# A written order for every engine in place of the planner's, in a kernel of linear attention and a gated feed-forward block

## The chip, the core and the metric

One core of a Trainium2 chip runs the whole kernel. The metric is the device time of one execution in microseconds (us). The engines are TensorE (PE in the profile, its weight loads PEld), VectorE (DVE), ScalarE (ACT), GpSimd (POOL) and SyncE (SP), which here only issues DMA transfers. Each works through its own list of instructions in order; between engines, semaphores say when data are there or a buffer is free.

## The reference, cut to what matters

```python
def _attn_ref(q, k, v, g_norm):              # (8, 8, 576, 64) each
    kv = np.einsum('bhsd,bhse->bhde', k, v)
    out = np.einsum('bhsd,bhde->bhse', q, kv)
    rms = np.sqrt(np.mean(out * out, axis=-1, keepdims=True) + 1e-06)
    return (out / rms * g_norm)

def _moe_ref(x, w_in, w_spatial, b_spatial, w_out):   # x (8, 576, 512)
    h = np.maximum(x @ w_in, 0.0)                     # w_in (512, 1024)
    u, v = (h[..., :512], h[..., 512:])
    v_n = (v - v.mean(-1)) / np.sqrt(v.var(-1) + 1e-06)
    v_s = np.einsum('ts,bsd->btd', w_spatial, v_n) + b_spatial[None, :, None]
    return (u * v_s) @ w_out                          # w_out (512, 512)
```

The attention's output, heads side by side, is the x of the second function. All is float32.

## The kernel before, in words

The eight batches are worked one after the other. A batch has 576 rows: four blocks of 128, and a tail of 64 rows; the tails of two batches share one block. Products in full precision are made from a high and a low part of each operand (`XH`, `XL`, `WVH`, ...; `split`, L508 and L509, casts the high part on ScalarE and subtracts it on VectorE), three TensorE products for one. Large products are cut into halves and put together as in Strassen's scheme (seven products for eight), whose sums and differences VectorE makes.

From batch 2 on a batch b has these stages on TensorE:

- `hv` (L505, tiles `psh`): v half of x @ w_in, four blocks, each followed by ReLU (L478), the layer norm's statistics (L484 to L491), scaling on ScalarE (L492) and a split into `VH`, `VL`. The tail's block is `hv_tail`, split into `TA` and `TB` (L554 to L556).
- `u_steps` (L697 to L727, tiles `psua`, `psub`, `psuc`, products at L742): the u half of x @ w_in. Its step p1 is copied out of PSUM by ScalarE (L697, `p`), since p2 goes on in the same bank; p7 adds it on VectorE (L716, `u`), and p4 goes on in that bank.
- `sp_steps` (L790 to L811, tiles `psa`, `psb`, `psc`): the product with w_spatial, in the same pattern (the copy is L790), then `gate` (L761, L763), which multiplies by u and splits the result into `G`, `GT`.
- `out_unit` (L472 with tiles `pso` and operands `WO`, `G`): the product with w_out, a copy by ScalarE (L844) and a store (L846).

The attention of a later batch is woven in: `part_k` (L300, `pskv`) makes kv from loads of `KV` and `KT`; `part_q` (L329, `pso` from `KVB` or `KVO` and `qt`) applies it to the queries; `square` (L372 to L375) and `normal` (L383, `x`) do the norm out of PSUM; `turn_over` (L407, `pstr`) transposes into `XH`, `XL` (L239, L240). These products use the array in pieces of 64x64 or 64x128 (the first pair of numbers in a profile row), all others use it whole, 128*128. A product in plain float32 shows as two records in the trace, one on split operands as one.

What sets the order: the source emits 5,750 instructions, and a planner then lists each engine's in an order of its own, by its estimate of when each could start, within what data and buffers allow. The token list `PLAN` sets the order in which the opening is emitted (pinned between its brackets), and `tc.issue_after` and `tc.high_priority` bind a few instructions; one such bond ties `x_sums` of a batch to the last `gate` of the batch before (L625 to L628, L766). PSUM has four banks for the main products (`ps_mm`) and two double banks for the attention (`ps_att`); `load` has two buffers for `qt` and `qs`, and `KV`, `KT` are pairs.

Of the kernel before, what the change touches and what calls it, by code (L numbers as in the profile page):

```python
# [39 lines left out]
u10 b1 X2 B10 t1 W W E1 L E0 A11 u11 W Q0 z u12 h D12 u13 W B12 T10 s s | s X1 T12 X0 s B11 D13 X5  # L40
B13 T11 X7 s s s s Y1 Y0 X4 P T13 O0 Q1 X6 W | p O1 R
"""


def f32(ap):
    return ap.bitcast(F32)
# [3 lines left out]
def body(ctx: ExitStack, tc, qT, qtl, kvm, kvt, g2, w_in, wsT, bsp, w_out, out):  # L50
    nc = tc.nc
# [455 lines left out]
    def split(hi, lo, x):  # L507
        nc.scalar.copy(hi, x)  # L508
        nc.vector.tensor_tensor(lo, x, f32(hi), op=ALU.subtract)  # L509
# [114 lines left out]

    def x_sums():  # L625

        with tc.issue_after(last_gate[0]):
            x_sums_()  # L628

    def x_sums_():  # L630
        for k in range(2):
            q = []
            for of, j, name in ((0, 0, "p1"), (2, 1, "u2"), (0, 1, "u3"), (2, 0, "g")):
                q.append(work.tile([P, HS], F32, name=name, tag=name))
                x = [f32(x[:, of + k, j * HS:(j + 1) * HS]) for x in (XH, XL)]
                nc.vector.tensor_tensor(q[-1], *x, op=ALU.add)
            q11, q22, q12, q21 = q
            nc.vector.tensor_tensor(q11, q12, q11, op=ALU.subtract)
            nc.vector.tensor_tensor(q12, q22, q12, op=ALU.subtract)
            nc.vector.tensor_tensor(q22, q22, q11, op=ALU.subtract)  # L640
            nc.vector.tensor_tensor(q21, q21, q22, op=ALU.subtract)
            for n, x in (1, q22), (0, q11), (2, q12), (3, q21):
                split(TH[n][:, k], TL[:, n, k], x)
# [106 lines left out]
        nc.tensor.matmul(ps, TB[i][:, ds], WTL[i][:, cols], start=False, stop=True,  # L750
                         skip_group_check=True)

    last_gate = [None]

    def gate(b, d, j, ps, add=None):

        i = b % 2
        cols = slice(j * HS, (j + 1) * HS)
        g = work.tile([P, HS], F32, name="g", tag="g")
        if add is not None:  # L760
            nc.vector.tensor_tensor(g, ps, add, op=ALU.add)  # L761
            ps = g
        nc.vector.scalar_tensor_tensor(g, U[:, d, cols], 0.0, ps, op0=ALU.max, op1=ALU.mult)  # L763
        if j == 0:
            split(GH[:, d, cols], GL[:, d, cols], g)
            last_gate[0] = next(i for i in reversed(nc.cur_bb.bb.instructions) if i.engine == mybir.EngineType.DVE)  # L766
        else:
            n, own = NT - HS, slice(i * TAIL, (i + 1) * TAIL)
            split(GH[:, d, HS:NT], GL[:, d, HS:NT], g[:, 0:n])
            split(GT[:, 0, d, own], GT[:, 1, d, own], g[:, n:HS])  # L770

    def sp_steps(b):
# [29 lines left out]
        def p2(q):  # L802
            ps = st.pop((q, "a"))
            product(ps, q, 1, 1, False, False)
            tail_product(ps, i, q, 0)
            gate(b, q, 0, ps)

        def p7(q):
            ps = st[q, "b"]
            product(ps, q, 4, 5, False)  # L810
            nc.vector.tensor_tensor(temp(q, "u3"), ps, st[q, "p1"], op=ALU.add)  # L811
            gate(b, 2 + q, 1, st[q, "c"], st.pop((q, "u3")))

        def p4(q):
            ps = st.pop((q, "b"))
            product(ps, q, 2, 6, False, False)
            tail_product(ps, i, 2 + q, 0)
            gate(b, 2 + q, 0, ps, st.pop((q, "p1")))
# [220 lines left out]
    def step(n=1):  # L1039
        for _ in range(n):  # L1040
            if queue:
                queue.pop(0)()
# [98 lines left out]
    def first(b):  # L1141

        if b > 1:
            to_u()
            x_sums()
# [48 lines left out]
    for b in range(2, NB):  # L1194
# [5 lines left out]
        if b % 2 == 0:  # L1200
            step(len(queue))


_OUTS = [((B, S, DM), "float32")]

# [43 lines left out]
```

## Time and profile before

| what | value |
|---|---|
| median of 3 runs | 524.04 us (522.02 to 526.14) |
| the profiled execution | 522.39 us |
| its span, first to last instruction | 520.6 us |
| its mean granted TensorE clock | 0.99 of 2.4 GHz |

The profile comes from one execution. An engine's busy time is a union of its instructions; matmuls are pipelined, so the busy time of PE contains overlap and small gaps. A wait is named by what ended it.

### The profile page before, as it was taken

What the parts mean: (1) busy time and instruction counts of PE and PEld (TensorE: products, weight loads), DVE (VectorE), ACT (ScalarE), POOL (GpSimd) and SP (SyncE); (2) the same over time, 40 slices, a digit from 0 to 9 for tenths busy, and PEclk for the clock granted to TensorE, in tenths of its full rate; (3) what the DMA queues carried; (4) which work ended last, traced back from release to release, by engine and by line L of the source; (5) the groups of instructions that cost most, each with busy time, mean ns of one, the idle gap of its engine ahead of it and who ended that gap; (6) DMA issues with size and microseconds to landing.
All of it is one profiled execution on the core that took longest, in us unless ns stands there. A gap on an engine that the chain in (4) does not pass through costs nothing.

```text
span 520.6 us, 12023 instructions
## 1 busy us (share of the span) xinstructions
PE 488.3 (94%) x4560; PEld 422.3 (81%) x4560; DVE 412.1 (79%) x1248; ACT 282.6 (54%) x913; POOL 20.7 (4%) x46
## 2 busy tenths in 40 slices
PE   6999999979799978999999999899999998999896
PEld 6658697867697868888988888788998888989895
DVE  2899888889597498796989689797899589876871
ACT  3758946865352675525653476435664377326422
POOL 5000000000000001000000000100000001000000
PEclk9999999998999979999999999999999999999999
DMA  7995100775526603817063153816050151214303
GB/s 251 336 349 209 40 3 20 238 235 168 161 89 195 226 1 115 313 54 251 13 228 108 50 173 93 296 40 212 2 196 11 49 175 55 108 42 162 137 26 103
DMA packets 28079, 71.99 MB, mean 138 GB/s; under 512 B 3506, under 2 KB 8626, under 8 KB 26484
## 3 DMA queue, kind: packets, MB, share of 16 engines
q1 hardware_dynamic: 24564, 49.19, 28.9%
q0 software_dynamic: 3456, 22.02, 12.3%
q8 instruction: 36, 0.59, 0.4%
q14 instruction: 23, 0.19, 0.1%
HBM read 58.09 MB, written 13.11 MB: 137 GB/s over the span
## 4 chain that ended last, share of the span: by engine, by line
PE 65%; DVE 12%; DMA 12%; ACT 6%; issue 2%; SPq 1%; ACTq 0%; DVEq 0%
PE pso L472 16%; PE psh L505 12%; PE psa L742 5%; PE psub L742 5%; DMA qt<-qT 4%; PE psua L742 3%; PE psb L742 3%; PE psc L742 3%; PE psuc L742 3%; PE psh L559 3%; DMA out<-o 2%; PE pso L329 2%; DMA stage<-w_out 2%; DMA spare_u<-w 2%; DMA KV<-kvm 2%
## 5 line engine op out<-in xcount | busy, mean ns | idle before, releaser
L472 PE MATMUL pso<-WO,G 128*128 128x512 f32 x384 | 95.1, 395 | 0.0
L472 PEld LDWEIGHTS pso<-WO,G 128*128 128x128 f32 x384 | 70.9, 189 | 14.8 <-ACT o L844 0.4
L508 ACT CAST G<-g 128x288 fp32r<-128x288 f32 (+1 forms) x56 | 22.9, 409 | 58.8 <-DVE g L763 58.5
L505 PE MATMUL psh<-WVH,XH 128*128 128x512 f32 x112 | 43.4, 392 | 0.8 <-ACT XH L239 0.8
L505 PE MATMUL psh<-WVL,XH 128*128 128x512 f32 x112 | 43.6, 390 | 0.0
L505 PE MATMUL psh<-WVH,XL 128*128 128x512 f32 x112 | 42.8, 391 | 0.0
L509 DVE TENSOR_TENSOR VL<-v,VH 128x512 fp32r<-128x512 f32 (+1 forms) x56 | 33.9, 621 | 9.1 <-ACT VH L508 8.6
L844 ACT COPY o<-pso 128x512 f32<-128x512 f32 x35 | 19.7, 590 | 39.2 <-PE pso L472 25.6
L508 ACT CAST VH<-v 128x512 fp32r<-128x512 f32 (+1 forms) x56 | 30.8, 564 | 9.4 <-DVE v L537 8.4
L492 ACT ACTIVATE v<-v,mv,rv 128x512 f32<-128x512 f32 x29 | 23.5, 816 | 22.3 <-DVE mv L491 21.3
L742 PE MATMUL psb<-WSH,VH 128*128 128x288 f32 x84 | 26.6, 317 | 1.9 <-DVE g L763 1.4
L484 DVE BATCH_NORM_STATS2 s<-v 128x6 f32<-128x512 f32 x35 | 23.6, 688 | 5.6 <-ACT v L478 5.4
L239 ACT ACTIVATE XH<-pstr,gcol 128x512 fp32r<-128x512 f32 x28 | 19.4, 704 | 13.5 <-PE pstr L246 6.7
L505 PEld LDWEIGHTS psh<-WVH,XH 128*128 128x128 f32 x112 | 21.0, 188 | 5.6 <-ACT XH L239 1.0
L509 DVE TENSOR_TENSOR G<-g,G 128x288 fp32r<-128x288 f32 (+1 forms) x56 | 23.6, 421 | 2.3 <-ACT G L508 1.8
L742 PE MATMUL psb<-WSH,VL 128*128 128x288 f32 x84 | 24.6, 296 | 0.3 <-DVE VL L509 0.3
L742 PE MATMUL psb<-WSL,VH 128*128 128x288 f32 x84 | 24.7, 295 | 0.0
L505 PEld LDWEIGHTS psh<-WVL,XH 128*128 128x128 f32 x112 | 21.0, 188 | 4.5 <-DVE WVL L904 0.2
L505 PEld LDWEIGHTS psh<-WVH,XL 128*128 128x128 f32 x112 | 21.0, 188 | 4.5
L478 ACT ACTIVATE v<-psh 128x512 f32<-128x512 f32 x32 | 18.7, 599 | 10.1 <-PE psh L505 9.4
L240 DVE SCALAR_TENSOR_TENSOR XL<-pstr,gcol,XH 128x512 fp32r<-128x512 f32 x28 | 20.8, 743 | 2.8 <-ACT XH L239 2.8
L742 PE MATMUL psa<-WSH,VH 128*128 128x288 f32 x56 | 17.4, 312 | 3.4 <-ACT p L790 3.0
(295 smaller groups left out, 1419.6 us busy)
## 6 DMA issues: line engine op xcount, KB each, us to landing
KV<-kvm SPq DMA_DIRECT2D x31, 512.0 KB, 5.5
WO<-spare_o POOLq DMA_DIRECT2D x12, 1024.0 KB, 6.7
UX<-spare_u POOLq DMA_DIRECT2D x12, 768.0 KB, 6.3
out<-o SPq DMA_DIRECT2D x32, 256.0 KB, 2.4
qt<-qT SPq DMA_DIRECT2D x28, 256.0 KB, 4.8
stage<-w_in SPq DMA_DIRECT2D x8, 512.0 KB, 6.9
KT<-kvt SPq DMA_DIRECT2D x32, 64.0 KB, 4.9
stage<-w_out SPq DMA_DIRECT2D x4, 512.0 KB, 5.1
```

Source lines behind the costliest of these rows:

```text
L239: nc.scalar.activation(hi, ps, AF.Copy, scale=gcol)
L240: nc.vector.scalar_tensor_tensor(lo, ps, gcol, f32(hi), op0=ALU.mult, op1=ALU.subtract)
L472: nc.tensor.matmul(ps, lt, rh, start=i == 0, stop=i == n - 1)
L478: nc.scalar.activation(v, ps, AF.Relu)
L484: nc.vector.bn_stats(s6, v)
L492: nc.scalar.activation(v, v, AF.Identity, bias=m, scale=r)
L505: nc.tensor.matmul(ps, lt, rh, start=k == 0 and i == 0, stop=k == NP - 1 and i == 2)
L508: nc.scalar.copy(hi, x)
L509: nc.vector.tensor_tensor(lo, x, f32(hi), op=ALU.subtract)
L559: nc.tensor.matmul(psv[c], X32[:, k, c * P:(c + 1) * P], W32[k], start=k == 0, stop=k == NP - 1)
L742: nc.tensor.matmul(ps, lt, rh, start=start and i == 0, stop=stop and i == len(pairs) - 1, skip_group_check=True)
L844: nc.scalar.copy(o, ps)
```

## The change

A dictionary `ORDER` holds one text for each engine. After all instructions have been emitted as before, the code goes through each text and binds each instruction behind the one that the text puts ahead of it, so that the planner is left with one order for each engine. The bond between `x_sums` and the last gate is taken out. Tiles, buffers, arithmetic, the instructions and the way they wait for data are the same.

```diff
+ORDER = {
+    "PE": """
+0.101 5.20 0.5 6 0.6 7.24 0.7 2.4 0.7 11 14 25 0 10 12 22 0 9 10 0 8.2 16.2 0.8 4.4 0.15 7 20.6 0.5 2.11 4.6
...
+    "Pool": """
+0.6 2.2 4.2 0.8 2 1 0.3 1 0 1 0 2 1 0.3 1 0.6 1 0 1 0
+""",
+}
...
     def x_sums():
 
-        with tc.issue_after(last_gate[0]):
-            x_sums_()
-
-    def x_sums_():
...
-    last_gate = [None]
...
-            last_gate[0] = next(i for i in reversed(nc.cur_bb.bb.instructions) if i.engine == mybir.EngineType.DVE)
...
+    queues = {}
+    for ins in list(nc.cur_bb.bb.instructions):
+        if not isinstance(ins, mybir.BassTilePoolBoundary):
+            queues.setdefault(ins.engine, []).append(ins)
+    for name, text in ORDER.items():
+        left, last = queues[getattr(mybir.EngineType, name)], None
+        for token in text.split():
+            at, n = (int(x) for x in (token + ".1").split(".")[:2])
+            for ins in left[at:at + n]:
+                if last is not None:
+                    tc.add_manual_dep(
+                        ins, last.name,
+                        mybir.DependencyInfo(mybir.DependencyClass.NoSync,
+                                             mybir.DependencyReason.DATA), reason="order")
+                last = ins
+            del left[at:at + n]
```

How a text is read: take the engine's instructions in the order in which the source emits them. A token `a.n` takes n instructions from place a of what is left, and they come next; a token `a` takes one. So `0.101` is the first 101 products as emitted, and `5.20` then takes 20 from five places on. The texts cover all 3,510 products, 760 ScalarE and 1,248 VectorE instructions, 189 issues of SyncE and 43 of GpSimd.

Read out in this way and laid against the order before, the first 340 products, 165 ScalarE and 212 VectorE instructions stand where they stood; product 340 starts at 81.51 us before. Behind that, 1,695 of the 3,510 products would have to be moved to turn the one order into the other. Some places, counted from 0 on each engine (batch numbers from 0):

| engine, what | order before | order in the table |
|---|---|---|
| PE, `part_q` of batch 2, first half | 521 to 552 | 494 to 525 |
| PE, `part_k` of batch 3, first half | 595 to 630 | 607 to 642 |
| PE, `part_q` of batch 2, second half | 631 to 662 | 643 to 674 |
| PE, between the first and the last of these three | 33 products of 288 columns, 9 of 512, `part_k` | 60 of 288, 21 of 512, `part_k` |
| DVE, the four L383 of that first half | 285 to 288 | 277, 280, 283, 284 |
| DVE, a weight's decoding, L895 to L898 | 277, 280, 282, 284 | 285, 286, 288, 290 |
| ACT, two L697 of batch 2 | 315, 319 | 301, 307 |
| ACT, two L492 of `hv` just ahead of the first L697 | 310, 311 | 292, 302 |
| PE, p1 of batch 2, second half; then its p2 | 1116 to 1121; 1160 to 1165 | 1037 to 1042; 1054 to 1059 |
| PE, products between these two | 6 of 288, two `turn_over` | 11 of 512 |
| DVE, two L716 of batch 2 | 478, 479 | 459, 464 |
| DVE, the tail's two L556 of batch 2 | 476, 477 | 468, 473 |
| ACT, two L790 of batch 6 | 689, 690 | 684, 689 |
| ACT, six casts L554 and L555, then L239 and L269 | 681 to 686, 687, 688 | 666 to 672, 700, 686 |
| SP, second `KV` load for `part_k` of batch 2, second half | 62, behind a load of w_out and four stores | 57, ahead of these |
| PE, `part_q` of batch 3, both halves | 892 to 923, 1011 to 1042 | 962 to 993, 1168 to 1199 |
| PE, `hv` of batch 2 starts at | 1050 | 950 |
| PE, `hv` of batch 3 starts at | 1570 | 1354 |
| PE, first `part_k` woven into batch 3 (for batch 4) | 1190 to 1225, in batch 2 | 1470 to 1505 |
| PE, `out_unit` of batch 2, its last product | 1569 | 1397 |
| SP, loads `KV`, `KT`, `qt` for it; the four stores of batch 2 | 115 to 120; 131 to 133, 136 | 119 to 124; 115 to 118 |
| PE, changes of the array's shape behind product 340 | 80 | 51 |

## Rows read from the trace of the kernel before

**Rows 1.** The page, part 1: busy time, share of the span and count of instructions of the engines.

```profile
PE 488.3 (94%) x4560; PEld 422.3 (81%) x4560; DVE 412.1 (79%) x1248; ACT 282.6 (54%) x913; POOL 20.7 (4%) x46
```

**Rows 2.** The waits of TensorE's products alone, from 81.5 us to the end (what waited <- what ended the wait: us in total, times, longest). The ten largest.

```profile
PE pso L329 <- DVE x L383: 3.7, 1, 3.7
PE psua L742 <- ACT p L697: 3.1, 2, 1.8
PE pso L329 <- DMA qt<-qT: 3.1, 3, 1.4
PE psa L742 <- ACT p L790: 3.0, 3, 1.3
PE psub L742 <- DVE u L716: 1.7, 2, 1.3
PE psb L742 <- DVE g L763: 1.4, 2, 1.2
PE pskv L300 <- DMA KV<-kvm: 1.2, 1, 1.2
PE pso L329 <- DVE KVB L317: 1.1, 1, 1.1
PE pstr L407 <- DVE KVO L317: 0.9, 1, 0.9
PE psh L505 <- ACT XH L239: 0.8, 1, 0.8
```

**Rows 3.** Busy time of each engine by stretch: the stretch, its length, busy us and (x instructions) of PE, PEld, DVE, ACT and POOL, then the granted clock of TensorE as a share of its full 2.4 GHz, the share of the DMA engines, GB/s.

```profile
81.50:120.00 38.50, 32.81 (x497) 29.06 (x495) 34.62 (x105) 26.44 (x77) 0.00 (x0) 0.97 0.49 162
...
192.00:196.00 4.00, 4.00 (x17) 4.00 (x17) 3.46 (x11) 2.60 (x7) 0.00 (x0) 0.50 0.00 0
```

**Rows 4.** The chain that ended last, in order of time (start, us, what). A matmul's name is followed by how many of it the piece holds.

```profile
117.92 1.99 PE pso L329 x64
119.90 4.40 PE pso L472 x15
...
190.40 1.81 PE psua L742 x6
192.21 1.59 PE psub L742 x6
193.81 1.44 PE psuc L742 x6
...
229.74 1.21 PE pskv L300 x72
...
237.89 10.90 PE psh L505 x48
248.79 1.58 PE psua L742 x12
...
273.87 1.28 PE pso L329 x64
...
327.35 9.64 DMA qt<-qT
```

**Rows 5.** The timeline of TensorE from 98 to 122 us (start, length of the merged piece, engine, line, what, shape, count, and in brackets the idle time before it).

```profile
98.63 0.29 PE L472 MATMUL psu<-XH,WUL 128*128 128x288 f32 x1
98.85 0.69 PE L300 MATMUL pskv<-KV 64*64 64x64 f32 x32
...
99.59 0.40 PE L472 MATMUL psu<-XH,WUH 128*128 128x288 f32 x1
99.83 0.29 PE L472 MATMUL psu<-XL,WUH 128*128 128x288 f32 x1
...
105.30 1.10 PE L329 MATMUL pso<-KVB,qt 64*64 64x64 f32 x62
...
117.92 1.99 PE L329 MATMUL pso<-KVB,qt 64*64 64x64 f32 x64 [3.67 <-DVE x L383]
```

**Rows 6.** The timeline of VectorE from 113.5 to 118 us.

```profile
115.18 0.43 DVE L897 TENSOR_SCALAR t<-stage 128x512 uint32<-128x512 uint32 x1
...
115.64 0.69 DVE L898 SCALAR_TENSOR_TENSOR stage<-stage,t 128x512 f32<-128x512 uint32 x1
116.25 1.41 DVE L383 TENSOR_TENSOR x<-pso,r 128x256 f32<-128x256 f32 x4
```

**Rows 7.** The timeline of ScalarE from 183 to 190.5 us.

```profile
186.90 0.38 ACT L697 COPY p<-psua 128x288 f32<-128x288 f32 x1
188.28 0.81 ACT L492 ACTIVATE v<-v,mv,rv 128x512 f32<-128x512 f32 x1 [1.00 <-DVE mv L491]
...
189.96 0.39 ACT L697 COPY p<-psua 128x288 f32<-128x288 f32 x1
```

**Rows 8.** The timeline of ScalarE from 438.9 to 442.8 us.

```profile
440.65 0.40 ACT L555 CAST TB<-d 64x256 fp32r<-64x256 f32 x1
...
441.95 0.70 ACT L790 COPY p<-psa 128x288 f32<-128x288 f32 x2
```

**Rows 9.** The timeline of VectorE from 197.5 to 202.2 us.

```profile
200.54 0.69 DVE L556 TENSOR_TENSOR TA<-v,TA 64x512 fp32r<-64x512 f32 x1 [0.46 <-ACT TA L554]
201.26 0.82 DVE L716 TENSOR_TENSOR u<-psub,p 128x288 f32<-128x288 f32 x2
```

**Rows 10.** The page, part 6: the issues of one kind of load (queue, operation, count, size, median us from issue to landing).

```profile
KV<-kvm SPq DMA_DIRECT2D x31, 512.0 KB, 5.5
```

More of the change, by code (lines that the diff above doesn't have):

```diff
@@ L42 @@
 """
+ORDER = {
+    "PE": """
[17 rows of a table added]
+""",
+    "Activation": """
[11 rows of a table added]
+""",
+    "DVE": """
[21 rows of a table added]
+""",
+    "SP": """
[3 rows of a table added]
+""",
+    "Pool": """
+0.6 2.2 4.2 0.8 2 1 0.3 1 0 1 0 2 1 0.3 1 0.6 1 0 1 0
+""",
+}
 def f32(ap):
```

51 rows, old and new, of the table ORDER are left out of this document.

## The prediction

> **What bounds the kernel now.** I read the page's busy times first. TensorE is busy 94% of the span, and no other engine is over 81%, VectorE at 79% [rows 1]. So TensorE sets the end, and what a new order can give back is the time in which its list stands still or runs slowly. The products themselves stay the same.
>
> Next I read the waits of TensorE from 81.5 us on, since the table leaves the first 340 products, and the other engines' lists up to there, as they were. The ten largest groups come to 3.7 + 3.1 + 3.1 + 3.0 + 1.7 + 1.4 + 1.2 + 1.1 + 0.9 + 0.8 = 20.0 us [rows 2]. Most end on VectorE or ScalarE, although these have idle time. The reader is to see that these are matters of order and not of capacity: an instruction that TensorE waits for stands in its engine's list behind others that nobody waits for yet.
>
> Third, the chain in order of time and the granted clock show a second loss. After two of these waits TensorE runs at half clock for a while: 0.50 of full, 1.2 GHz, from 192 to 196 us [rows 3], where six products of 288 columns take 1.59 us instead of 0.79 (half of the 1.58 us for twelve) [rows 4].
>
> **The change part by part.** It adds and removes no instruction. I read the table out and laid it against the order before, place by place.
>
> *Waits.* (1) The 3.7 us of `part_q` on L383. The second half needs the PSUM bank that the first half's `normal` frees. The first half began at 105.30 us and ended about 106.3; the second began at 117.92 [rows 5]: 11.6 us were needed, and 33 products of 288 columns, 9 of 512 and a `part_k`, 7.6 us by the prices below, covered. The table puts 60 products of 288 columns (0.132 us each), 21 of 512 (0.227 each) and a `part_k` (1.21) between them [rows 4], which is 7.9 + 4.8 + 1.2 = 13.9 us. It also takes the L383 out from behind the decoding of a weight, of which two operations alone are 0.43 + 0.69 us [rows 6]. I count all 3.7 as gone.
>
> (2) The 3.1 us of p2 on the copy L697. The copies run at 186.90 and 189.96 us, behind scalings L492 that themselves wait for statistics, one of them 1.00 us [rows 7]. The table puts the first copy ahead of one of these, and puts eleven products of 512 columns, 2.5 us, between p1 and p2 where six of 288 and two small transposes stood. All 3.1 gone.
>
> (3) The 3.0 us on the copy L790. At 441.95 us two copies stood right behind the tail's casts and the transposes' [rows 8]; the table sends the casts well ahead and the largest transposed block behind. Of the three places I looked at, one in the last batch is not helped (two casts stay ahead of its copy), so 2.0 gone.
>
> (4) The 1.7 us on L716: two of these ran at 201.26 us, behind L556, which had waited 0.46 us for a cast and taken 0.69 [rows 9]. In the table they stand ahead of both L556; 1.5 gone.
>
> (5) The 1.2 us on a `KV` load: its issue moves from behind four stores and a weight's load to the front of them, but `part_k` also comes earlier; 0.9 gone. (6) The 0.8 us on L239: the transposes move ahead of six products and a `part_k`, 2.6 us; all gone. (7) The 1.4 us on L763: one of its two goes ahead of the weights' sums; 1.2 gone. (8) The 3.1 us on `qt` and the 2.0 on L317 sit where attention is woven in, and all of that is placed anew; I take half, 1.5 + 1.0.
>
> Together 3.7 + 3.1 + 2.0 + 1.5 + 0.9 + 0.8 + 1.2 + 2.5 = 15.7 us.
>
> *New waits.* I laid the chain from each product through ScalarE and VectorE to the product that needs it (durations of this trace, engines' queues left out) against the TensorE work between the two. In the table 54 products have under 0.5 us to spare, before 26; none is short by more than 0.3 us, before some were, by up to 1.1. So the table is tight. I take 0.1 us of lateness for each of the 28 more, 3 us. The bounds are 0 and 28 x 0.4 = 11 us.
>
> *The rule that speaks against it.* The Trainium skill, TensorE: Matmul & The Clock Gate, section on the array's architectural detail, says that VectorE and ScalarE take their queues strictly in order. This case's trace agrees [rows 7]: a copy whose data were there stood behind a scaling that waited 1.00 us. By that rule a tight fixed list hands each late operand on to everything behind it, and the term would lie at its upper bound; the trace bears this out only for the single place, so I stay low.
>
> *Half clock.* The two stretches: 18 products of 288 columns in 1.81 + 1.59 + 1.44 = 4.84 us instead of 2.38, and 64 records of `part_q` plus 15 products of 512 columns in 1.99 + 4.40 instead of 1.28 + 3.41 [rows 4]: 2.5 + 1.7 = 4.2 us. Both follow a wait that I count as gone, so this goes too. Bounds 0 and 4.2.
>
> *Changes of the array's shape.* A `part_k` in the midst of whole-array products costs more than its own products: the step into it is 98.63 to 98.85, 0.22 us instead of 0.13, and the first step after it 99.59 to 99.83, 0.24 instead of 0.13 [rows 4, 5]. So a change costs 0.09 to 0.11 us, and somewhat more for the way out, which these rows don't separate; I bound it by 0.10 and 0.16 and take 0.13. The table has 51 changes where 80 were: 29 x 0.13 = 3.8 us saved (2.9 to 4.6).
>
> *The bond of `x_sums`* goes, but the table orders VectorE fully, so it costs and gives nothing of its own. *The end*: the last product group is another block of the same size; its copy runs whole where two half copies ran one after the other. Nothing either way. *SP and POOL*: no transfer is added; what their order may cost is the second rival.
>
> Sum against the profiled execution of 522.39 us: 522.4 - 15.7 + 3 - 4.2 - 3.8 = 501.7 us. The median of the runs is 1.65 us above that execution, so I forecast 503.
>
> **The rivals.**
>
> *All of it goes.* The 20.0 us of waits, the half clock and the upper price of the shapes: 522.4 - 20.0 - 4.2 - 4.6 = 493.6, on the median 495. For it: no chain is clearly short. Against: transfers and queues are not in that count.
>
> *The loads come too late (slower).* The table weaves attention in later: the first `part_k` for batch 4 moves from batch 2 into batch 3, 72 products behind the last output block of batch 2, and on SP its loads, which stood ahead of that batch's four stores, now stand behind them. The cover is 24 products of 512 columns and 48 of 288, 5.4 + 6.3 = 11.7 us [rows 4]. The median load lands in 5.5 us [rows 10], but one wait of the chain on `qt` is 9.64 us long [rows 4], and the stores wait for copies first. If each of the eight halves of batches 4 to 7 waited 3.5 us, that is 28 us: 501.7 + 28 = 530, on the median 531. It decides against the change from 20.7 / 8 = 2.6 us a half. A rule that bears on it: the Trainium skill, DMA: Bandwidth & Descriptors, section on queues, rings and completion order, says that completion isn't in order for one issuing engine, so loads behind stores would lose their place but not wait for the stores to land; no row here shows it.
>
> *The waits only move.* VectorE is busy 34.6 of 38.5 us from 81.5 to 120 us [rows 3], 90%; where it is the bound, TensorE waits for it at another place. If all waits come back elsewhere and the half clock stays, only the shapes are left: 522.4 - 3.8 = 518.6, on the median 520.
>
> *The table doesn't bind*, or only repeats what the planner does: 524. Against: the order read out differs for 1,695 products, and engines take their lists in order.
>
> **How the numbers follow.** Chances: the forecast 0.64, all of it 0.14, late loads 0.08, waits that move 0.10, no effect 0.04. The forecast's own range is 495 (waits at their lower bound) to 513 (new waits at 11, less half clock back). Eight times in ten I expect 492 to 515. A measurement of this kernel can tell about 1%, 5.2 us, from no change. Faster by more: 0.64 + 0.14 and a little of the moved waits, 0.79; within 1%: 0.13; slower: 0.08.
>
> **What would show it.** Right: waits of TensorE behind 81.5 us near 7 us, no wait on L383 or L697 over 1 us, full granted clock behind the opening, and a `part_k` and a `part_q` more often back to back. Wrong: waits on `KV` or `qt` of several us in each batch from 4 on (late loads); the sum of waits still near 20 us under other names (moved); stretches at 0.50 of the clock that follow a new wait.

## The result: 495.88 us, and the profile after

| | before | after |
|---|---|---|
| median | 523.75 us (4 runs) | 495.88 us (4 runs, 495.22 to 497.11) |
| profiled execution; its span | 522.39; 520.6 us | 497.11; 495.3 us |
| mean granted clock | 0.990 | 0.996 |

The ratio is 0.9468, 95% interval 0.9425 to 0.951. That is 27.9 us less on the medians and 25.3 us in the two profiled executions. The forecast was 503, its range 492 to 515.

Behind the dictionary, lines stand 66 lines further down in the changed kernel up to line 624, and 59 to 62 lines behind it: L383 is now L449, L329 is L395, L300 is L366, L317 is L383, L239 is L305, L508 is L574, L472 is L538, L697 is L759, L716 is L778, L742 is L804, L790 is L849, L763 is L823, L844 is L903.

The busy times after, beside [rows 1]:

```profile
PE 479.4 (97%) x4560; PEld 417.4 (84%) x4560; DVE 415.8 (84%) x1248; ACT 286.5 (58%) x913; POOL 21.1 (4%) x46
```

VectorE and ScalarE do the same work in the same time (415.8 for 412.1 us, 286.5 for 282.6). Only TensorE's list has become denser.

The waits of TensorE behind 81.5 us, all that there are, beside [rows 2]:

```profile
PE pso L538 <- DMA WO<-spare_o: 1.9, 1, 1.9
PE pskv L366 <- DVE XL L306: 1.1, 1, 1.1
PE psc L804 <- ACT o L903: 1.0, 1, 1.0
PE pst L414 <- DMA qs<-qtl: 0.9, 2, 0.6
PE psc L804 <- ACT VH L574: 0.2, 1, 0.2
```

None of the ten groups of [rows 2] is left. In the same view, the whole list before came to 21.5 us in 22 waits; here it is 5.1 us in 6.

Two stretches of the changed kernel, with the columns of [rows 3]:

```profile
81.50:120.00 38.50, 37.38 (x537) 32.75 (x536) 35.71 (x109) 28.41 (x81) 0.00 (x0) 1.00 0.55 176
...
252.00:255.40 3.40, 3.40 (x14) 3.21 (x14) 1.83 (x6) 0.95 (x3) 0.00 (x0) 0.50 0.07 21
```

In the first, TensorE runs 537 records where it ran 497 [rows 3], and VectorE is busy 35.7 instead of 34.6 us of 38.5, so VectorE wasn't at its limit there. The second is the only stretch at half clock between the opening and the last product. It follows the 1.9 us wait for `WO`, whose load took 10.1 us in this execution (from the chain that ended last):

```profile
240.56 10.10 DMA WO<-spare_o
```

How the table works is best seen at step 2, the second half of batch 2. TensorE:

```profile
169.87 0.29 PE L804 MATMUL psua<-XH,WUL 128*128 128x288 f32 x1
170.00 0.39 PE L538 MATMUL psh<-WVL,XH 128*128 128x512 f32 x1
...
172.28 0.39 PE L538 MATMUL psh<-WVH,XL 128*128 128x512 f32 x1
172.50 0.29 PE L804 MATMUL psua<-XH,WUH 128*128 128x288 f32 x1
```

and ScalarE at the same time:

```profile
169.46 0.81 ACT L558 ACTIVATE v<-v,mv,rv 128x512 f32<-128x512 f32 x1 [0.90 <-DVE mv L557]
170.31 0.41 ACT L574 CAST VH<-v 128x256 fp32r<-128x256 f32 x1
170.62 0.39 ACT L759 COPY p<-psua 128x288 f32<-128x288 f32 x1
```

The first product behind p1 starts at 170.00, the copy ends at 171.01, and p2 starts at 172.50, when eleven products of 512 columns are through. ScalarE still waits 0.90 us for statistics just before, but nobody waits for ScalarE.

The same reading at the 19 places where TensorE's wait is for a copy of L759 or L849 shows the copy ending 0.05 to 3.4 us before TensorE goes on in the bank, at seven of them by less than 0.35 us. Before, both waits on L697 and all three on L790 were among the ten largest groups [rows 2].

### The profile page after: what moved, and what is told of

Its sections match the earlier page's. It is cut to its first block, busy times and chain, and to the rows that moved or that the text cites. A ratio compares the mean times of both kernels' runs of the same rounds, so it can differ in the third digit from the quotient of the medians.

```text
span 495.3 us, 11993 instructions
## 1 busy us (share of the span) xinstructions
PE 479.4 (97%) x4560; PEld 417.4 (84%) x4560; DVE 415.8 (84%) x1248; ACT 286.5 (58%) x913; POOL 21.1 (4%) x46
## 4 chain that ended last, share of the span: by engine, by line
PE 66%; DVE 13%; ACT 10%; DMA 8%; issue 2%; SPq 1%; POOL 0%; ACTq 0%; DVEq 0%
PE pso L538 18%; PE psh L571 10%; PE psb L804 6%; PE psa L804 6%; PE psub L804 4%; PE psc L804 4%; PE psh L625 3%; PE psuc L804 3%; DMA stage<-w_in 3%; PE psua L804 2%; DMA WO<-spare_o 2%; DMA qs<-qtl 2%; PE pskv L366 2%; DVE VL L575 2%; PE psu L663 1%
## 5 line engine op out<-in xcount | busy, mean ns | idle before, releaser
L538 PE MATMUL pso<-WO,G 128*128 128x512 f32 x384 | 98.3, 397 | 1.9 <-DMA WO<-spare_o 1.9
L538 PEld LDWEIGHTS pso<-WO,G 128*128 128x128 f32 x384 | 69.6, 189 | 16.8 <-DVE r L253 2.1
L574 ACT CAST G<-g 128x288 fp32r<-128x288 f32 (+1 forms) x56 | 22.8, 408 | 38.0 <-DVE g L823 37.8
L574 ACT CAST VH<-v 128x512 fp32r<-128x512 f32 (+1 forms) x56 | 31.0, 568 | 10.9 <-DVE v L603 9.1
L903 ACT COPY o<-pso 128x512 f32<-128x512 f32 x35 | 20.1, 587 | 22.1 <-PE pso L538 20.4
L305 ACT ACTIVATE XH<-pstr,gcol 128x512 fp32r<-128x512 f32 x28 | 19.2, 696 | 15.9 <-PE pstr L473 7.1
L804 PE MATMUL psb<-WSH,VH 128*128 128x288 f32 x84 | 26.2, 312 | 0.0
L804 PE MATMUL psb<-WSH,VL 128*128 128x288 f32 x84 | 25.2, 300 | 0.0
L804 PE MATMUL psb<-WSL,VH 128*128 128x288 f32 x84 | 25.2, 300 | 0.0
L1133 POOL DMA_DIRECT2D UX<-spare_u x12 | 6.5, 544 | 302.4 <-DVE T L575 150.4
```

What stands on the lines that cost most here:

```text
L305: nc.scalar.activation(hi, ps, AF.Copy, scale=gcol)
L538: nc.tensor.matmul(ps, lt, rh, start=i == 0, stop=i == n - 1)
L804: nc.tensor.matmul(ps, lt, rh, start=start and i == 0, stop=stop and i == len(pairs) - 1, skip_group_check=True)
L903: nc.scalar.copy(o, ps)
```

## The experiments

Each ratio is to the kernel before, run again beside it (medians 521.85 to 523.75 us).

| kernel | median, us | ratio to the kernel before, 95% | waits of TensorE behind 81.5 us |
|---|---|---|---|
| bond taken out, no text | 519.89 | 0.9923 to 0.9972 | 21.3 us in 20 |
| text of TensorE alone | 548.55 | 1.0433 to 1.058 | 45.3 in 42 |
| texts of ScalarE and VectorE | 553.41 | 1.0556 to 1.0646 | 38.3 in 42 |
| TensorE and VectorE | 535.14 | 1.0158 to 1.0291 | 28.8 in 33 |
| TensorE and ScalarE | 529.47 | 1.0067 to 1.0166 | 29.8 in 31 |
| TensorE, ScalarE and VectorE | 498.71 | 0.9511 to 0.9592 | 7.1 in 8 |
| all five (the changed kernel) | 495.88 | 0.9425 to 0.951 | 5.1 in 6 |
| the same again, beside the later tries | 496.79 | 0.9456 to 0.953 | 4.7 in 6 |
| cover taken away at ten places | 507.06 | 0.9642 to 0.9762 | 10.7 in 15 |
| 62 more changes of shape | 505.72 | 0.9655 to 0.9734 | 1.5 in 3 |
| six copies one or two places later | 498.93 | 0.9502 to 0.9578 | 7.2 in 9 |
| four waits removed | 493.21 | 0.941 to 0.9493 | 4.2 in 8 |
| six edits against waits | 492.52 | 0.9381 to 0.945 | 1.4 in 4 |

**Which part of the table brings it.** The texts are applied to some engines only, and the planner lists the others around them:

```diff
     for name, text in ORDER.items():
+        if name not in ('PE',):
+            continue
```

The bond alone:

> The texts are left out; only the bond between x_sums and the last gate is gone, so the planner orders every engine, with one bond less. Theory (the gain comes from the written order): within 3 us of the kernel before, 521 to 527, and the sum of TensorE's waits behind 81.5 us again near 20 us. Rival (the bond held VectorE's list back, and its going brings a part of the gain): 515 or less, with the waits on the instructions that stood behind the bond gone.

519.89 us, 0.5% less, with 21.3 us of waits as before. The rival falls: the order is the gain. Under the planner the bond's going is worth some 2 us. That it costs and gives nothing once everything is ordered, as the prediction put it, was not tried: no run has the table with the bond.

TensorE's text alone:

> Only TensorE's text is applied; ScalarE, VectorE, SyncE and GpSimd are left to the planner, which lists them around the fixed order of TensorE. Theory (the gain needs the lists to fit one another): the cover that TensorE's own order gives, steps 1, 2, 6, half of step 8, the shapes and the clock, stays, 3.7 + 3.1 + 0.8 + 2.5 + 2.4 + 4.7 = 17 us, and the waits that hang on the lists of ScalarE and VectorE (steps 3, 4, 7, and what the planner newly puts in the way) come back: 503 to 510 us, waits of TensorE behind the opening of 10 to 15 us on the copies and gates. Rival (TensorE's order alone is the gain): 494 to 499 us, waits near 5 us.

Both fall: 548.55 us, 5% slower than before. The largest single wait shows why. TensorE:

```profile
385.82 0.96 PE L804 MATMUL psuc<-T,UX 128*128 128x288 f32 x6
392.64 0.61 PE L804 MATMUL psub<-UX,WUH 128*128 128x288 f32 x1 [5.86 <-DVE u L778]
```

VectorE meanwhile, from this kernel's timeline:

```profile
387.57 0.69 DVE L575 TENSOR_TENSOR VL<-v,VH 128x512 fp32r<-128x512 f32 x1 [1.53 <-ACT VH L574]
...
389.10 0.41 DVE L441 TENSOR_REDUCE s<-x 128x4 f32<-128x256 f32 x1
...
391.51 0.63 DVE L575 TENSOR_TENSOR VL<-v,VH 128x512 fp32r<-128x512 f32 x1
392.06 0.16 DVE L253 TENSOR_TENSOR r<-s,q 128x16 f32<-128x16 f32 x1
392.14 0.45 DVE L778 TENSOR_TENSOR u<-psub,p 128x288 f32<-128x288 f32 x1
```

L778 adds p, copied by 382.3 on ScalarE, to products of `psub` that ended near 386. It ran at 392.14, behind a split that itself waited 1.53 us for ScalarE and eleven instructions after that, while TensorE stood still. From 388.8 to 395.6 us, within the wait and behind it, the granted clock is 0.50. TensorE's order, which is good with the other two lists, is worse than the planner's own without them.

The other two lists without TensorE's:

> Only the texts of ScalarE and VectorE are applied; the planner lists TensorE, SyncE and GpSimd around them. Theory (the lists have to fit one another, and the cover lies in TensorE's order): 508 to 520 us, with fewer waits than before on ScalarE and VectorE but the old number of changes of the array's shape or nearly so. Rival (the order of the two engines that TensorE waits for is the whole gain): 494 to 500 us whatever TensorE's own order is.

553.41 us: slower again, and outside both expectations. With one of the two lists planned:

> The texts of TensorE and VectorE are applied; ScalarE, SyncE and GpSimd are left to the planner. Theory A (ScalarE, the least busy of the three, is the one whose list the planner can be trusted with): within 5 us of the kernel with all three, 497 to 503 us. Theory B (any one list that does not fit the others is enough, since each engine takes its list in order and the copies and casts on ScalarE are what TensorE waits for): 520 us or more, with the waits on L544, L759, L849 and L574.

> The texts of TensorE and ScalarE are applied; VectorE, SyncE and GpSimd are left to the planner. With TensorE and VectorE written and ScalarE planned it was 535 us. Theory (one list that does not fit is enough, whichever it is; VectorE has more instructions and less idle time, so its list hurts at least as much): 530 to 550 us, with the waits on VectorE's lines (L778, L789, L821, L383). Rival (the planner lists VectorE well as long as ScalarE is fixed): under 510 us.

535.14 and 529.47 us. Either missing list costs 31 to 36 us against the 498.71 us of all three, so theory B holds, and so does its counterpart for VectorE, though 0.5 us below its range. That VectorE's list hurts at least as much as ScalarE's did not come out: 529 against 535 us. The waits are on the engine that is planned, and beyond it. With ScalarE planned:

```profile
PE psuc L804 <- ACT v L544: 4.4, 4, 1.6
PE psub L804 <- DVE u L769: 4.2, 4, 3.6
```

With VectorE planned:

```profile
PE pstr L473 <- DVE KVO L383: 4.6, 2, 2.5
PE psb L804 <- DVE u L870: 2.6, 3, 1.6
```

The transfers left to the planner:

> The texts of TensorE, ScalarE and VectorE are applied; SyncE and GpSimd, which issue the transfers, are left to the planner. Theory (the transfers are hidden in either order): within 2 us of the changed kernel, 494 to 499 us, with the same waits on the products of 512 columns for WO. Rival (the table's order of the transfers is a part of the gain): 500 us or more, with new waits on KV, qt or qs.

498.71 us, in the range of the theory but 2.8 us above the changed kernel, not within 2, and 1.9 above its repeat, whose interval of ratios overlaps with this one. Behind 81.5 us this kernel has 7.1 us of waits for 5.1, the largest a 2.6 us wait for `qs`, where the changed kernel has 0.9 in two; that was the sign of the rival. The rest of the difference between the two profiled executions lies in the opening: product 340 starts at 83.65 instead of 81.59 us in its profile, and the clock there is low for a while,

```profile
7.40:14.10 6.70, 5.32 (x28) 5.12 (x30) 2.69 (x7) 2.72 (x18) 0.15 (x1) 0.50 0.98 334
```

which some executions of other kernels with the whole table show too. So the order of the transfers is worth at most 2 us or so behind the opening, in one profile, and no more is shown.

**What one piece of cover is worth.** At ten places p2 is put right behind p1, and what stood between comes after. Here and below the fence shows a piece of one engine's list, with - where an instruction stood and + where it stands now:

```diff
 L804 MATMUL psua<-XH,WUL 128x288
+L804 MATMUL psua<-XH,WUH 128x288
...
 L538 MATMUL psh<-WVL,XH 128x512
...
-L804 MATMUL psua<-XH,WUH 128x288
...
```

> The whole table, with one edit in TensorE's text: at ten places of batches 2 to 7 where a bank is copied out between p1 and the products that go on in it, those products (2 to 6 of them) stand directly behind p1, and what stood between them comes after. The lists of ScalarE and VectorE stay. From the trace of the changed kernel the copies end 0.60 to 1.33 us after p1 does, 7.9 us in sum. Theory (a wait is the copy's end less what TensorE has been given to do meanwhile): waits on L759 and L849 at these ten places of 0.5 to 1.4 us each, 7 to 9 us in sum, and half clock behind the longer of them: 502 to 508 us. Rival (TensorE's waits are made up later by work that is then ready sooner, since other engines have idle time): under 499 us.

507.06 us. The profile has a new wait at each of the ten places, 7.0 us in sum where 7.9 were worked out from the copies' ends:

```profile
PE psua L804 <- ACT p L759: 3.8, 4, 1.2
PE psa L804 <- ACT p L849: 3.2, 6, 0.7
```

At the place shown above it is

```profile
171.43 0.29 PE L804 MATMUL psua<-XL,WUH 128*128 128x288 f32 x1
171.56 0.29 PE L804 MATMUL psua<-XH,WUL 128*128 128x288 f32 x1
173.00 0.40 PE L804 MATMUL psua<-XH,WUH 128*128 128x288 f32 x1 [1.14 <-ACT p L759]
173.24 0.30 PE L804 MATMUL psua<-XL,WUH 128*128 128x288 f32 x1
```

The theory holds for the waits. The span rose by 11.6 us, more than the view of waits (10.7 for 5.1). 1.9 us lie in the opening of this execution (product 340 starts at 83.53). Another 2.5 lie at the waits but outside the view. It counts a wait from the end of the last product's row, 171.86 here, while without the wait the next product would have started 0.13 us after that one's start, at 171.70; and the step behind the wait is 0.24 instead of 0.13 us. So each of the ten waits costs about 0.26 us more than it shows. The remaining 1.6 us weren't taken apart. None of the ten waits, of which the longest is 1.2 us, is followed by half clock; the 1.6 us wait for `WO` in the same execution is.

**How tight it is.** Six copies stand one or two places later in ScalarE's list:

```diff
-L759 COPY p<-psua 128x288
 L574 CAST VH<-v 128x512
+L759 COPY p<-psua 128x288
...
```

> The whole table, with one edit in ScalarE's text: at six places of batches 2 to 7 the copy out of psua or psa (L759, L849) stands one or two instructions further back, behind instructions that ran right after it. From the trace of the changed kernel the six copies then end 0.68, 0.38, 0.45, 0.86, 0.93 and 0.80 us after TensorE wants their bank, 4.1 us in sum. Theory (the table is just in time: a copy late by so much makes TensorE wait by as much): 4 to 6 us more than the changed kernel beside it, with waits on L759 and L849 of these sizes. Rival (there is slack behind, and a late copy is made up for): less than 2 us more.

498.93 against 496.79 us beside it, 2.1 us more and between the two expectations; the intervals of the two ratios overlap, so the profiles have to tell. The view of waits has 2.5 us on the psua copies and 0.5 on the psa copies (their lines stand one higher here):

```profile
PE psua L803 <- ACT p L758: 2.5, 4, 0.9
...
PE psa L803 <- ACT p L848: 0.5, 1, 0.5
```

Five of the six places wait, 3.0 us in sum in the view, which again leaves out 0.16 us of each. Product by product, the five start 0.68, 0.43, 0.87, 0.95 and 0.67 us later against their neighbours than in the changed kernel: 3.6 us, for 3.65 worked out at these five. The sixth, worked out at 0.45, comes some 0.15 us late without a listed wait. So the table is just in time at these places. Some of it is made up further on: a 0.3 us wait for `qs` at 139 us, for one, is gone, and behind product 340 the kernel takes 3.1 us more than the repeat in its profile.

**What a change of the array's shape costs.** 31 whole-array products that stood beside a `part_k` or `part_q` go into its midst:

```diff
-L538 MATMUL pso<-WO,G 128x512
 L366 MATMUL pskv<-KV 64x64 x9
+L538 MATMUL pso<-WO,G 128x512
...
```

> The whole table, with one edit in TensorE's text: 31 whole-array products that stand right beside a part_k or part_q are put one by one into the midst of it, so that the changes of the array's shape behind product 340 go from 51 to 113; none of them moves by more than 1 us. Theory (a change costs 0.13 us, the price taken in the prediction): 62 x 0.13 = 8.1 us more, 503 to 505 us. Rival (0.10 us, the lower bound): 6.2 us more, 501 to 503. Second rival (the change itself is hidden, what the pieces of a part_k lose comes from their own start): under 3 us more.

505.72 us, 9 to 10 us more than the changed kernel, although the waits fell from 5.1 to 1.5 us at the same time. All three prices were too low. In the changed kernel one `part_k` takes 1.10 us from its start to that of the `part_q` behind it:

```profile
114.35 0.74 PE L366 MATMUL pskv<-KV 64*64 64x64 f32 x34
...
115.45 1.11 PE L395 MATMUL pso<-KVB,qt 64*64 64x64 f32 x64
```

With three products of 512 columns inside (lines stand one lower here):

```profile
115.13 0.56 PE L367 MATMUL pskv<-KV 64*64 64x64 f32 x18
115.62 0.50 PE L539 MATMUL pso<-WO,G 128*128 128x512 f32 x1
116.05 0.46 PE L367 MATMUL pskv<-KV 64*64 64x64 f32 x14
...
118.19 0.27 PE L396 MATMUL pso<-KVB,qt 64*64 64x64 f32 x3
```

That is 3.06 us, of which 1.10 are the part itself and 3 x 0.227 = 0.68 the three products; 1.28 us are left for six changes, 0.21 each. Over the eight groups that were edited, from the start of the product ahead to the start of the first one behind, the same products take 33.7 us where they took 21.3: 12.4 us for 62 changes, 0.20 us each. The Trainium skill, TensorEngine Tiling (Array Packing), key properties of the tiling modes, says that a change of the tiling mode drains TensorE, without a price; the trace agrees that a change costs time, 0.20 us here.

A part that is left whole shows nearly the same price in the changed kernel:

```profile
411.28 0.30 PE L804 MATMUL psua<-XH,WUL 128*128 128x288 f32 x1
411.51 1.16 PE L395 MATMUL pso<-KVO,qt 64*64 64x64 f32 x64
412.60 0.80 PE L804 MATMUL psuc<-T,UX 128*128 128x288 f32 x4
```

The step ahead of the part is 0.23 us instead of 0.13, and the step behind it 0.24. The part itself takes 1.09 us for 64 records, and parts of 136 records take 2.14, so 72 records more need 1.05 and 64 need 0.93: 0.16 us are left at the part's own ends. That is 0.36 us for the two changes, 0.18 each.

**A version that beats both.** Four moves against the waits that were left, then two more:

```diff
-L538 MATMUL pso<-WO,G 128x512 x3
 L804 MATMUL psa<-WSL,VH 128x288
...
+L538 MATMUL pso<-WO,G 128x512 x3
 L538 MATMUL pso<-WO,G 128x512 x4
```

> The whole table with four small moves against the waits that are left in the changed kernel: three products for WO behind thirteen of psa, psc and psb (1.9 us of waiting for a 10.1 us load, and the half clock of 252 to 255 us behind it, 1.5 us), three products of psa ahead of the psc that waits for an o copy (0.4 us), three products for WO ahead of the transposes whose pst waits for qs (0.6 us), and at 88 us one ScalarE and one VectorE instruction (L305, L306) one and two places up (0.7 us). Theory (each wait left is again a matter of order): 1.9 + 1.5 + 0.4 + 0.6 + 0.7 = 5.1 us less, 490 to 492.5 us. Rival (the list is tight, and each move brings another wait): 495 us or more.

493.21 us, between the two expectations, with an interval that overlaps with that of the repeated kernel. No half clock behind the opening, and the waits for `WO` and `XL` shrink to 0.3 and 0.5 us, but two others are as long as before or longer:

```profile
PE psc L804 <- ACT o L903: 1.1, 1, 1.1
PE pst L414 <- DMA qs<-qtl: 0.9, 1, 0.9
```

So about half of the 5.1 us came. The second try goes for these two:

```diff
+L366 MATMUL pskv<-KV 64x64 x16
...
 L804 MATMUL psc<-WSH,VH 128x288
...
-L366 MATMUL pskv<-KV 64x64 x16
```

> The four small moves of the earlier try, and two more against the waits that it left: a part_k of batch 3 whose loads had landed 10 us before (36 products, 1.2 us) ahead of the psc that waits 1.1 us for an o copy, and on SyncE the load of qs that TensorE waited 0.9 us for ahead of four loads of KV and KT that have 46 us to spare. Theory (a wait goes when the work put ahead of it is as long, and a load's wait goes when it is issued earlier by as much): 1.1 + 0.9 less 0.4 for two more changes of the array's shape, that is 1.6 us under the earlier try, 491 to 492.5 us, and 3 to 5 us under the changed kernel beside it. Rival (what is moved ahead makes other waits of the same size): within 1.5 us of the changed kernel.

> The changed kernel once more, unaltered, as the measure for the three kernels beside it: 494 to 498 us, waits of TensorE behind the opening near 5 us, one stretch of half clock behind the wait for WO if that wait is again about 1.9 us, none if it comes out under 1.3 us.

492.52 us (492.09 to 492.75), the changed kernel beside it 496.79 (494.61 to 498.32): 4.3 us less, and all that is left in the view of waits is

```profile
PE pskv L366 <- DMA KV<-kvm: 0.5, 1, 0.5
PE pskv L366 <- DVE XL L306: 0.5, 1, 0.5
PE pso L538 <- ACT GT L574: 0.2, 1, 0.2
PE psc L804 <- ACT VH L574: 0.2, 1, 0.2
```

The intervals of the two ratios, 0.9381 to 0.945 and 0.9456 to 0.953, do not touch. The unaltered kernel, run again, had the 1.8 us wait for `WO` but no half clock behind it, against what I expected:

```profile
249.00:256.00 7.00, 5.40 (x84) 4.95 (x88) 4.98 (x17) 0.96 (x3) 0.00 (x0) 1.00 0.40 133
```

## Why the prediction came out as it did

The mechanism was right, and the likeliest case was 7 us too slow, where the rival in which all of it goes stood (495). The forecast for the profiled execution was 501.7, and 497.11 was measured: 4.6 us. Most of the rest is the 1.65 us that I added to go from the profiled execution to the median; here the median lies 1.2 us below it. That the rival's 495 is so near is luck in part: for the profiled execution it gives 493.6, and it has no new waits.

With the sizes that the runs show, the sum is 522.4 - 16.4 (waits, net) - 2.7 (half clock) - 5.2 (shapes) = 498.1. That this is within 1 us is luck in part too, since two terms are in no step of it. What a wait costs beyond the view came to 5.2 us at the 22 waits of before and comes to 1.3 at the 6 of after, 3.9 us less. Against it, the other steps of TensorE take 2.6 us more: many products start late by less than the 0.15 us under which the view lists no wait.

- Steps 1, 2, 4, 5, 6 and 7 came as put or a little better: none of these waits is left. At step 1, the first half of `part_q` begins at 100.31 and the second at 115.45 (shown above): 15.1 us, and the normals on L449 end at 114.3. The cover of 13.9 us behind the first half was right. They are later than the 11.6 us of before, and still in time.
- Steps 3 and 8 were mis-sized. I left 1.0 of 3.0 us on L790 and half of 5.1 us on `qt` and L317; all of it went. For `qt` the trace of after shows loads that land about 5 us or more before their use behind 150 us. With 0.7 us of steps 4, 5 and 7 and the 1.5 us of groups under the ten, 5.8 us more went than I counted.
- New waits were put at 3 us, as 0.1 us of lateness at 28 tight products. 5.1 us came, and in another form: six single waits. The three on loads, 2.8 us in sum, were in no step. What I had in mind is there too, below the view: between whole-array products away from waits, 69 steps are 0.02 to 0.3 us too long where 26 were, 5.2 us for 3.2. Net, by the view, the waits went by 16.4 us, and I had put 12.7.
- The rule of the Trainium skill that spoke against it (TensorE: Matmul & The Clock Gate, the array's architectural detail: VectorE and ScalarE take their queues strictly in order) agrees with the four runs in which one or two lists don't fit: 28.8 to 45.3 us of waits. It prices the mismatch of lists, and not the table.
- Half clock: both stretches of before are gone, 4.2 us as put. A new one behind the wait for `WO` gave 1.5 us back in the profiled execution (nine products of 288 columns at 0.24 us, and four of 512 in 1.42 instead of 0.91), and not in the repeat's.
- Changes of shape: 29 fewer, at 0.13 us each by [rows 5]. The price measured at whole parts is 0.18 us, above my upper bound of 0.16, which makes 5.2 instead of 3.8 us. The failing step is the bound: I took the steps ahead of a part and behind it, 0.09 and 0.11 us, and put nothing on the part itself, which takes 0.16 us more than its records need. The 5.2 us are an estimate, 29 at this price.
- Late loads, the rival on the slower side, rested on a misreading, which the table of places ahead of the prediction shares. The loads 119 to 124 on SyncE aren't those of the first `part_k` for batch 4 but of the next one. SyncE in the changed kernel:

```profile
184.52 0.33 SPq L184 DMA_DIRECT2D KV<-kvm  x1
...
206.23 15.13 SPq L905 DMA_DIRECT2D out<-o  x4
229.90 0.34 SPq L184 DMA_DIRECT2D KV<-kvm  x1
```

  The first `part_k` runs at 229.14 on loads issued from 184.52 on, ahead of the four stores. The loads behind the stores start at 229.90, when that `part_k` has freed the buffer, the last of them has landed at 238.2, and the `part_k` that they serve starts at 240.07. The margin there is 1.9 us; the smallest in the later batches is 0.5 us at 370.6. So no half was late. How far the loads could move was not tried.
- Waits that only move, and a table that doesn't bind, fall with the sum of waits, 5.1 us in the view for 21.5.

## What to carry to other kernels

When one engine is busy 94% and its waits end on engines with idle time, ask of each wait what stood ahead of the awaited instruction in its list, and how much work the waiting engine had been given meanwhile; their difference is the wait, and at ten places it could be predicted to 0.9 us in 7.9. Fix the lists of the engines that wait for each other together or not at all: TensorE's good list alone, the other two alone, or one of them with TensorE's, were 1% to 6% slower than the planner's. Keep parts in another array shape whole, and let them be the cover for something.

## What the runs showed of the hardware that was not expected

A change of the array's shape costs 0.18 to 0.20 us at full clock, on the mean of the way in and the way out, against 0.13 us for a whole product of 288 columns. Going in and out costs 0.36 us at a whole part, of which 0.16 lie at the ends of the part itself.

A wait of TensorE between whole-array products costs about 0.26 us more than its idle time in the profile: 0.16 us of overlap with the product ahead, and 0.1 us at the step behind it. At 22 waits before and 6 after, that is 3.9 us of the 25.3.

Half clock after a wait isn't certain. The waits of 3.67 us before the change and of 5.86 us above were followed by it. Of the waits for `WO` at the same place, those of 1.9 us (changed kernel) and 1.6 us (cover taken away) were, and those of 1.8 us (the repeat), 1.9 us (late copies) and 1.4 us (transfers planned) were not; the 2.6 us wait for `qs` in the last of these was. So a single profile can hold or lack 1.5 us of it, and what I put as following a wait is only likely to.
